# Forward and backward of four layers on one core: sweeps in alternating direction, three blocks kept in SBUF, and two turns of layer 2 done by DMA

## The chip, the core and the metric

The kernel runs on one core of a Trainium2 chip. Its time is the device time of one execution in microseconds. Of the kernel before, 8 runs are shown: median 1104.16 us, from 1103.3 to 1107.43.

## The reference

A network of four layers is applied to x (2048 tokens of 512 channels, bf16), and then the gradients of its input and of all five weights are computed from grad_out. The layers are A, B, A, B with the same weights for both As and both Bs; each adds its result to x. In the kernel they are layers 0, 1, 2 and 3.

```python
def _A_ref(x, wqkv, wo):          # 32 heads of 16 channels
    q, k, v = qkv[0], qkv[1], qkv[2]
    phi = lambda t: jnp.where(t > 0, t + 1, jnp.exp(t)) + 1e-6
    pq, pk = phi(q), phi(k)
    kv = jnp.einsum("bhsd,bhse->bhde", pk, v)
    z = jnp.einsum("bhsd->bhd", pk)
    num = jnp.einsum("bhqd,bhde->bhqe", pq, kv)
    den = jnp.einsum("bhqd,bhd->bhq", pq, z)[..., None] + 1e-6
    return (num / den) @ wo
def _B_ref(x, w_gate, w_up, w_down):   # 1376 hidden channels
    return (_sigmoid(x @ w_gate) * (x @ w_up)) @ w_down
x = x + _A_ref(_layernorm(x), ...); x = x + _B_ref(_layernorm(x), ...)   # twice
```

Two properties set the shape of the kernel. An A layer needs sums over all tokens (kv and z) before any token can go on, and so does its backward pass. So the tokens have to be walked through several times.

## The kernel before, in words

The 2048 tokens are cut into 8 blocks of 256. Five sweeps walk over the blocks, and a last stage computes the weight gradients:

1. Sweep 1: layer norm of layer 0 (h), K and phi(K), the sums G = h'pk and z, and Q (`a_k`, `a_q`). A barrier (`a_barrier`) forms kv and the matrix Wp = kv times wo.
2. Sweep 2: the second half of layer 0 (`a_p2`: 1/den, the normalised pnT = phi(q)/den, then ya = pn Wp), layer 1 (`glu_fwd`), and layer norm, K and sums of layer 2. A barrier again.
3. Sweep 3: Q of layer 2 and its second half (`a_p2`), layer 3 forward and backward together (`glu_both`), and the first backward half of layer 2 (`a_b1`: it needs the gradient dx turned, so that channels lie on partitions; dpn = gradient times WpT, and the sum M over all tokens). A backward barrier (`a_bbarrier`).
4. Sweep 4: the second backward half of layer 2 (`a_b2`), the backward pass of layer 1 (`glu_bwd`), the first backward half of layer 0.
5. Sweep 5: the second backward half of layer 0.
6. `dw`: gradients of the weights, as long products over all tokens (dw_ps).

All sweeps walk the blocks from 0 to 7. What a later sweep needs is stored to DRAM by block and loaded again: the f32 stream (xf_d loaded as x2l, dxa_d as dxal, dxb_d as dxbl), h, phi(k), pnT, rphiT (the derivative of phi over den), dqT, dkT.

The order of the instructions isn't that of the code. Each step is registered as a piece in a planner (`Plan`, lines 75 to 270) with its dependencies, the tokens (buffers) it takes and gives back, and an estimated cost on each engine; hand-set offsets (OFFSETS, lines 284 to 295) shift its priority. The planner runs the pieces against its own clock, and the order in which it starts them becomes each engine's order, which the chip follows: an instruction that isn't ready stops all that stands behind it on its engine. All DMAs are issued by SyncE (SP) in one such order. Pools limit what may lie in SBUF: t2 has 20 buffers of 256 KB (128x1024 bf16), xb has 5 of 512 KB (a block of the f32 stream), w4 7, w11 6; in PSUM there are five mm tiles, two acc tiles and one tp tile.

There are two ways to turn a tile. `add_turn` (line 484) turns half a block by four transposes on TensorE into PSUM (line 479) and one copy by ScalarE (line 481). `load_turn` (line 498) reads from DRAM with a transposing DMA.

1/den of a block lies as 128 tokens x 32 heads (`den`, line 806). Before the change VectorE writes it as two bf16 parts into rr (lines 822, 824), TensorE turns it (`turn`, line 826) and spreads each head's row over its 16 channels by a product with a constant matrix (`spread`, line 834, r_ps), and VectorE multiplies from PSUM: pnT = pqT times r (line 844) and rphiT (lines 847, 849). ya_ps (line 856) waits for both halves of pnT.

Further lines that matter: hTq is the turned h of layer 2 that Q of blocks 2 to 7 uses, loaded at line 773 (Q of blocks 0 and 1 uses the tile that K had). The gradient of layer 2 is cast by ScalarE (line 905) and turned by `add_turn` (line 943); dpn_ps (line 914) uses it, m_ps (line 963) doesn't. dha_ps (line 1129) uses dqTl. The backward layer norm `ln_bwd` (line 1058) is one step on ScalarE, one on VectorE, one on GpSimd (ab, line 1070) and two more on VectorE. wgT is loaded at lines 1486 and 1487; lines 1471 and 1488 clear the unused rows of wd, wuT and wgT on GpSimd.

Of the kernel before, what the change touches and what calls it, by code (L numbers as in the profile page):

```python
# [74 lines left out]
class Plan:  # L75
# [11 lines left out]
    RATE = 0.27  # L87
# [17 lines left out]
    def load(self, key, fn, mb, deps=(), use="", pull=0.0):  # L105
        self.add(key, fn, 0.0, deps, [("D", mb / self.RATE)], use, pull=pull)

# [172 lines left out]
ACCJ, ACCY = 11, 7  # L280
SUMS = {1: ([0, 1], -1), 3: ([2, 3], 1), 5: ([4, 5], 3), 6: ([6], 5), 7: ([7], 6)}
# [3 lines left out]
    CB1:1=-7 DE0:1=-63,2=-19,4=+5,7=+5 DE2:1=-23 DK0:2=+1,4=+21 DP0:0=+36,1=-28,2=+36,3=+36,5=-102 DP2:2=+63,6=-51  # L285
    DT0:+83 DW1:0=-30 DW3:1=+1,7=-2 E3:0=-31,1=+2 G11:0=-7,6=+24,7=+66 G3:1=+1 GS0:3=+31,5=-1,6=-86 GS2:5=+7,6=+44
    J0:1=-74 K0:3=-12 K2:0=+28,1=+28,2=+28,3=+28,4=+29,6=+44,7=+10 LB2:1=-93 LB3:2=-52,3=-12,6=+63,7=+106 LDH0:0=-49
    LDH2:3=+97 LDL0:0=+53,2=+38 LDP0:1=-6 LDP2:3=+41 LDQ0:3=+67 LDX0:0=+113 LDX2:1=-102,2=-13 LG3:0=+7 LH1:6=-75
    LN0:1=-131,5=-68,6=+58 LN2:0=-1 LP0:7=-44 LS1:1=-57 MS0:5=-40 MS2:1=-12,5=-34,7=-87
    Q0:1=-103,2=-115,4=-101,5=-22 Q2:0=-1,1=-23,2=+8 RT0:2=+7 RT2:2=+47 S0:+44 S2:-3 SG2:-64 SH1:2=+17 SN0:4=+50  # L290
    SP0:0=-66 SP2:1=-6,5=-11,7=+1 SPREAD:-24 SQ2:0=+2,6=-77 SU1:3=+1,6=-21 SV1:0=-15,3=+22,6=-13
    TG0:0=+6,1=+3,2=+7,4=+3,5=-18 TG2:6=+38 TK0:2=+113,5=+22,6=+48 TK2:7=+55 TR1:3=-11 UT0:2=-98,3=+2 WGT:-26
    WPL0:+56 WT0:0=-35,1=-40 Y33:7=-97 YA2:5=-43 ZE0:0=+1,3=-2 ZE2:2=+16,4=+19,6=+151 ZS0:5=-8,7=+136 ZS2:7=-52
    ZZ0:+35
# [7 lines left out]
def kernel(  # L302
# [38 lines left out]
    k.rphi_d = {l: dt_(f"rphi_d{l}", [D, S]) for l in (0, 2)}  # L341
# [156 lines left out]
def load_turn(k, key, src, put, name, deps, pull=0.0):  # L498

    def ld():  # L500
        t = t2(k, name)
        put(t)
        k.nc.sync.dma_start_transpose(out=t[:], in_=src)
    k.G.load(f"{key}.0", ld, BLK, deps, "+t2", pull)
    k.G.add(f"{key}.1", lambda: None, 0.0, [f"{key}.0"])


def layernorm(k, l, b, x_fn, deps, sums=False):

    nc, G = k.nc, k.G  # L510

    def half_sums(j):
# [3 lines left out]
        col = slice(2 * b + j, 2 * b + j + 1)  # L516
        rs, sx = k.rstd[l][:, col], k.sx[l][:, col]
# [18 lines left out]
    def half(j):  # L536
# [3 lines left out]
        col = slice(2 * b + j, 2 * b + j + 1)  # L540
# [24 lines left out]
    G.store(f"SH{l}.{b}", lambda: nc.sync.dma_start(out=tok3(k.h_d[l], b), in_=k.h[l, b][:]), BLK, [f"LN{l}.{b}.{j}@h" for j in range(2)])  # L565
# [15 lines left out]
def a_k(k, l, b, keep, by_dma=False):  # L581
# [3 lines left out]
    n = f"{l}.{b}"  # L585

# [9 lines left out]
    if by_dma:  # L596
        load_turn(k, f"TK{n}", k.h_d[l][brows(b), :], put, "hTk", [f"SH{n}"])
    else:
        add_turn(k, f"TK{n}", lambda: k.h[l, b], put, "hTk", [[f"LN{n}.{j}@h"] for j in range(2)])
# [5 lines left out]
    G.store(f"SPK{n}", lambda: nc.sync.dma_start(out=tok3(k.pk_d[l], b), in_=A.pk[b][:]), BLK, [f"K{n}.{j}" for j in range(2)])  # L605
# [160 lines left out]
def a_q(k, l, b, keep, deps):  # L766
    nc, G = k.nc, k.G
    A = k.A[l]
    n = f"{l}.{b}"

    def ld():
        A.hT[b] = t2(k, "hTq")
        nc.sync.dma_start_transpose(out=A.hT[b][:], in_=k.h_d[l][brows(b), :])

    def half(hf):
# [3 lines left out]
        for c2 in range(2):  # L779
            for m in range(NDC):  # L780
                nc.tensor.matmul(ps[:, c2, :], lhsT=k.wq[:, m, cslice(2 * hf + c2)], rhs=A.hT[b][:, m, :],  # L781
                                 start=(m == 0), stop=(m == NDC - 1))
        yield
        yield from phi(k, flat(A.pq[b][:, 2 * hf:2 * hf + 2, :]), flat(ps[:]))
    if keep:
        src = [f"TK{n}.0", f"TK{n}.1"]
    else:
        G.load(f"LQ{n}", ld, BLK, [f"SH{n}", f"<K{n}.1"] + deps, "+t2")
        src = [f"LQ{n}"]
# [3 lines left out]
    G.free("-t2", [f"<Q{n}.1", f"<K{n}.1"])  # L793


def a_p2(k, l, b, xin_fn, deps, late):
# [4 lines left out]
    n = f"{l}.{b}"  # L801

# [3 lines left out]
    def den():  # L806
# [9 lines left out]
        yield  # L816
        r = k.p1.tile([P, 2, H], F32, name="rcp", tag="rcp", bufs=2)
# [8 lines left out]
    def turn():  # L826
# [5 lines left out]
        nc.vector.tensor_copy(st["rT"][:], flat(tps[:]))  # L832

# [17 lines left out]
    def y(j):  # L851
# [3 lines left out]
        for c in range(NDC):  # L855
# [4 lines left out]
    G.load("LX" + n, lx, BLK if l == 0 else 2 * BLK, [f"YA{l}.{b - 2}.1", f"SX{l - 1}.{b}"] + deps, "+t2" if l == 0 else "+xb")  # L860
    G.add("DE" + n, den, 8 * 0.027, [f"Q{n}.0", f"Q{n}.1", f"ZZ{l}", f"<YA{l}.{b - 2}.1"],
          [("V", 0.22, "+dn -tp"), ("V", 0.55), ("V", 0.2, "+rr"), ("V", 0.22, "-dn")], "+tp")
    G.add("RT" + n, turn, 2 * C128, ["DE" + n, "SPREAD"] + late, [("V", 0.29, "-tp +rT")], "+tp -rr")
    for hf in range(2):
        G.add(f"SP{n}.{hf}", lambda hf=hf: spread(hf), 2 * C256, ["RT" + n] + ([f"<SP{n}.0"] if hf else []),
              [("V", 0.68, "@pn"), ("V", 0.29, "+s1"), ("V", 0.68, "-s1 -mm")], "+mm" if hf else "+mm +t2 +t2")
    pn = [f"SP{n}.{hf}@pn" for hf in range(2)]
    G.free("-rT", [f"<SP{n}.1"])
    G.free("-t2", [f"SP{n}.0", f"SP{n}.1"])
    G.store(f"SN{n}", lambda: nc.sync.dma_start(out=dmaj(k.pnT_d[l], b), in_=A.pn[b][:]), BLK, pn)  # L870
    G.store(f"SR{n}", lambda: nc.sync.dma_start(out=dmaj(k.rphi_d[l], b), in_=A.rphi[b][:]), BLK, [f"SP{n}.{hf}" for hf in range(2)], "-t2")
# [10 lines left out]
def a_b1(k, l, b, deps):  # L882

    nc, G = k.nc, k.G
# [22 lines left out]
    def dpn(hf):  # L907
# [31 lines left out]
    G.load("LN_" + n, ldt, BLK, [f"SN{n}", f"<MS{l}.{b - 2 if b % 2 else b - 3}.3", f"<DP{l}.{b - 2}.0"] + deps, "+t2")  # L939
# [3 lines left out]
    add_turn(k, f"TG{n}", lambda: st["g"], lambda t: st.__setitem__("gT", t), f"gT{l}", [[f"CA{n}.{j}"] for j in range(2)], pull)  # L943
# [8 lines left out]
    G.store(f"SQ{n}", lambda: nc.sync.dma_start(out=dmaj(k.dqT_d[l], b), in_=st["dq"][:]), BLK, [f"ZE{n}.{hf}" for hf in range(2)], "-t2")  # L952
    if b in MSUMS:
# [26 lines left out]
        G.free(" ".join(["-t2"] * 2 * len(bs)), [f"<MS{n}.3"] + [f"<TG{l}.{bb}.1" for bb in bs])  # L980
# [104 lines left out]
def a_b2(k, l, b, x_load, out, deps, out_use=""):  # L1085
# [4 lines left out]
    n = f"{l}.{b}"  # L1090

# [3 lines left out]
    def ldt(nm, src):  # L1095
        st[nm] = t2(k, nm)
        nc.sync.dma_start_transpose(out=st[nm][:], in_=src[brows(b), :])

    def ldq():
        st["dqT"] = t2(k, "dqTl")  # L1100
        nc.sync.dma_start(out=st["dqT"][:], in_=dmaj(k.dqT_d[l], b))

    def ldh():
        st["h"] = t2(k, "hl", [P, 2, D])
        nc.sync.dma_start(out=st["h"][:], in_=tok3(k.h_d[l], b))
# [26 lines left out]
    G.load("LDH" + n, lambda: ldt("hT", k.h_d[l]), BLK, pre, "+t2")  # L1132
    G.load("LDP" + n, lambda: ldt("pkT", k.pk_d[l]), BLK, pre, "+t2")
    G.load("LDQ" + n, ldq, BLK, pre + [f"SQ{n}"], "+t2")
    G.load("LDL" + n, ldh, BLK, pre, "+t2")
    G.load("LDX" + n, ldx, 2 * BLK, pre + [f"SDX{l + 1}.{b}"], "+xb")
# [4 lines left out]
    G.store(f"SK{n}", lambda: nc.sync.dma_start(out=dmaj(k.dkT_d[l], b), in_=st["dkT"][:]), BLK, [f"DK{n}.{hf}" for hf in range(2)])  # L1141
# [3 lines left out]
    add_lnb(k, l, b, lambda j: (st["ps", j][:], st["h"][:, j, :], st["x"][:, j, :], out(st["x"], j)),  # L1145
            [[f"DH{n}.{j}", "LDL" + n, "LDX" + n] for j in range(2)], "mm", out_use)
    G.free("-t2 -t2", [f"<DH{n}.1"])
# [40 lines left out]
def glu_fwd(k, l, b):  # L1188
# [3 lines left out]
    n = f"{l}.{b}"  # L1192
    x = k.x
# [35 lines left out]
    for p in range(NPAIR):  # L1229
# [5 lines left out]
        G.add(f"Y{n}.{p}", lambda p=p: y(p), q * 2 * C512, [f"G{n}.{p}@hh", "WD"] + ([f"<Y{n}.{p - 1}"] if p else []),  # L1235
              [("V", 0.77, "-acc @0"), ("V", 0.77, "-acc")] if p == NPAIR - 1 else [], "" if p else "+acc +acc")
    G.free("-t2", [f"<G{n}.5"])
    G.store("SHH" + n, lambda: store_hh(k, k.hh_d[l], b, st["hh"]), HHB, [f"G{n}.{p}@hh" for p in range(NPAIR)])
    G.store("SS" + n, lambda: nc.sync.dma_start(out=k.s2t_d[b], in_=st["s2t"][:].rearrange("p a c t -> p (a c t)")), 2 * HHB,
            [f"G{n}.{p}" for p in range(NPAIR)], "-w11")  # L1240
    G.store("SX" + n, lambda: nc.sync.dma_start(out=tok3(k.xf_d, b), in_=x[0, b][:]), 2 * BLK, [f"Y{n}.5"])
# [13 lines left out]
def add_dh(k, l, b, st, src):  # L1255
# [8 lines left out]
    for p in range(NPAIR):  # L1264
# [4 lines left out]
        G.store(f"SU{n}.{p}", lambda p=p: store_pair(k, k.du_d[l], b, p, st["pair"][p][0][:]), mb, [f"{src}{n}.{p}@u"])  # L1269
        G.store(f"SV{n}.{p}", lambda p=p: store_pair(k, k.dg_d[l], b, p, st["pair"][p][1][:]), mb, [f"{src}{n}.{p}"])  # L1270
# [3 lines left out]
def glu_both(k, l, b):  # L1274
# [57 lines left out]
    G.load("LG" + n, lg, BLK, [f"<G{l}.{b - 2}.5"] + (["WWD"] if early else [f"<G{l}.{b - 1}.2"]), "+t2")  # L1332
# [18 lines left out]
    add_dh(k, l, b, st, "G")  # L1351
# [482 lines left out]
```

## Time and profile before

| | us |
|---|---|
| median of 8 runs | 1104.16 |
| the profiled execution, its own time | 1104.03 |
| its span, from first to last instruction | 1102.2 |
| TensorE busy in the span | 1074.4 |
| mean granted TensorE clock | 0.998 |
| DMA queue q1, share of 16 engines | 86.8% |

The span is cut into stages where the work changes: sweep 1 to about 44 us, the turnover to sweep 2 to 68 us, sweep 2 to 235 us, the turnover to sweep 3 to 257 us, sweep 3 to 533 us, sweep 4 to 742 us, sweep 5 among weight gradients to 884 us, and weight gradients alone to the end. A row of the profile gives a group of instructions with its count, busy time and mean duration; the duration of a product on TensorE contains its pipeline, so that products which follow each other overlap, and the distance of their starts is what one costs. A line of waits names the engine and line that waited, who released it, the total in us, how often, and the longest. Idle time of an engine that is not the bottleneck costs nothing.

### The profile page before, as it was taken

The page shows a single profiled execution, that of the slowest core. Times are in us where ns is not written, and L with a number is a line of the kernel's source. Part 1 is how long each engine was busy: PE and PEld are TensorE (multiplying, and loading weights), DVE is VectorE, ACT ScalarE, POOL GpSimd, SP SyncE. Part 2 cuts the span into 40 slices and gives each one's busy share as a digit, 9 for nine tenths or more (in the row PEclk, how much of TensorE's full clock was granted, in tenths as well). Part 3 has the DMA queues.
Part 4 walks back from the last instruction along what each step waited for, and adds up shares of the span by engine and source line. Part 5 has one row for each costly group of instructions (what it writes and reads, how often), then busy time and mean ns, then how long its engine had stood idle before and what let it go on. Part 6 is the DMA issues. An engine that isn't in the chain of part 4 may idle for free.

```text
span 1102.2 us, 20100 instructions
## 1 busy us (share of the span) xinstructions
PE 1074.4 (97%) x7561; PEld 710.5 (64%) x7660; DVE 656.2 (60%) x1613; ACT 366.1 (33%) x733; POOL 154.8 (14%) x435
## 2 busy tenths in 40 slices
PE   7999999989999999999999999999999999999998
PEld 4667676667666666776665656665554456666787
DVE  6798978688776789767957576767755000000010
ACT  7655454455343334433244534341111000000010
POOL 4146564313121002000001000000000000000000
PEclk9999999999999999999999999999999999999999
DMA  7728996997788678865999999979999999999960
GB/s 246 252 81 277 241 311 190 305 200 187 201 211 178 178 190 208 188 168 152 272 250 255 244 261 280 252 202 255 257 251 271 268 227 227 221 252 222 208 148 20
DMA packets 490339, 242.72 MB, mean 220 GB/s; under 512 B 296225, under 2 KB 474625, under 8 KB 488193
## 3 DMA queue, kind: packets, MB, share of 16 engines
q1 hardware_dynamic: 490240, 241.43, 86.8%
q8 instruction: 60, 0.98, 0.4%
q14 instruction: 39, 0.31, 0.1%
HBM read 68.75 MB, written 100.43 MB: 153 GB/s over the span
## 4 chain that ended last, share of the span: by engine, by line
PE 90%; DMA 4%; DVE 3%; ACT 2%; issue 1%; SPq 0%; POOL 0%; ACTq 0%; DVEq 0%
PE dw_ps L1716 25%; PE dh_acc L1251 7%; PE g_ps L1181 7%; PE u_ps L1181 7%; PE dhh_ps L1181 6%; PE dha_ps L1129 6%; PE dh_acc L1249 6%; PE y_ps L1370 3%; PE y_acc L1222 3%; PE dpn_ps L914 2%; PE ya_ps L856 2%; PE m_ps L963 2%; PE k_ps L592 2%; PE q_ps L781 2%; PE dpk_ps L1113 2%; PE g_ps L618 2%
## 5 line engine op out<-in xcount | busy, mean ns | idle before, releaser
L1716 PE MATMUL dw_ps<-dw_set,h 128*128 128x352 bf16 (+2 forms) x1536 | 205.6, 297 | 0.0
L1716 PEld LDWEIGHTS <-h 128*128 128x128 bf16 x1536 | 150.3, 98 | 55.3
L1698 DVE TENSOR_SCALAR dw_o<-dw_ps 128x512 bf16<-128x512 f32 (+3 forms) x33 | 17.6, 540 | 234.0 <-PE dw_ps L1716 214.5
L1251 PE MATMUL dh_acc<-wgT,dg 128*128 128x512 bf16 x349 | 132.3, 379 | 1.9
L1249 PE MATMUL dh_acc<-wuT,du 128*128 128x512 bf16 x317 | 120.1, 379 | 0.2
L1696 ACT ACTIVATE dw_o<-dw_ps 128x512 bf16<-128x512 f32 (+4 forms) x34 | 16.2, 480 | 245.9 <-PE dw_ps L1716 211.0
L1181 PE MATMUL u_ps<-hT,wu 128*128 128x256 bf16 x704 | 92.5, 273 | 0.0
L1181 PE MATMUL g_ps<-hT,wg 128*128 128x256 bf16 x704 | 92.5, 272 | 0.0
L1181 PE MATMUL dhh_ps<-gT,wdT 128*128 128x256 bf16 x704 | 89.0, 274 | 0.9 <-ACT gT L481 0.7
L1070 POOL TENSOR_SCALAR ab<-c 128x2 f32<-128x2 f32 x64 | 18.6, 291 | 446.7 <-DVE lnb_j L1067 441.9
L1181 PEld LDWEIGHTS <-wg 128*128 128x128 bf16 x704 | 68.1, 98 | 20.3
L1716 PE MATMUL dw_ps<-g,dw_set 128*128 128x512 bf16 (+1 forms) x343 | 77.3, 379 | 3.2 <-DMA dw_set<-hh_d 1.6
L1181 PEld LDWEIGHTS <-wdT 128*128 128x128 bf16 x704 | 68.6, 98 | 12.8 <-issue 1.2
L1181 PEld LDWEIGHTS <-wu 128*128 128x128 bf16 x704 | 68.9, 98 | 8.0
L1716 PEld LDWEIGHTS <-dw_set 128*128 128x128 bf16 (+1 forms) x352 | 35.1, 100 | 42.1 <-DMA dw_set<-hh_d 1.9
L1251 PEld LDWEIGHTS <-dg 128*128 128x128 bf16 x352 | 34.4, 98 | 33.4
L1249 PEld LDWEIGHTS <-du 128*128 128x128 bf16 x352 | 34.4, 98 | 33.4
L1064 ACT ACTIVATE lnb_t<-dha_ps,rstd 128x512 f32<-128x512 f32 x32 | 22.0, 688 | 83.9 <-PE dha_ps L1129 49.4
L481 ACT COPY gT<-gT_ps 128x512 bf16<-128x512 bf16 x48 | 28.2, 587 | 59.8 <-PE gT_ps L479 58.3
L1304 ACT ACTIVATE th<-g_ps 128x512 f32<-128x512 f32 (+1 forms) x48 | 26.8, 557 | 53.7 <-PE g_ps L1181 47.2
L1211 DVE SCALAR_TENSOR_TENSOR hh<-th,u_ps 128x512 bf16<-128x512 f32 (+1 forms) x48 | 30.4, 638 | 19.7 <-ACT th L1206 13.7
L1222 PE MATMUL y_acc<-wd,hh 128*128 128x512 bf16 x165 | 41.5, 379 | 0.6
(201 smaller groups left out, 1840.9 us busy)
## 6 DMA issues: line engine op xcount, KB each, us to landing
s2t_d<-s2t SPq DMA_DIRECT2D x8, 1408.0 KB, 6.6
s2tl<-s2t_d SPq DMA_DIRECT2D x8, 1408.0 KB, 8.1
hh_d<-hh SPq DMA_DIRECT2D x16, 640.0 KB, 4.6
du_d<-du SPq DMA_DIRECT2D x80, 128.0 KB, 2.9
dg_d<-dg SPq DMA_DIRECT2D x80, 128.0 KB, 2.7
h_d<-h SPq DMA_DIRECT2D x32, 256.0 KB, 2.9
h<-h_d SPq DMA_DIRECT2D x18, 256.0 KB, 4.9
pk_d<-pk SPq DMA_DIRECT2D x16, 256.0 KB, 2.6
```

The source lines that it names most:

```text
L481: nc.scalar.copy(dst[:, :, tslice(j)], ps[:])
L592: nc.tensor.matmul(ps[:], lhsT=A.hT[b][:, m, tslice(j)], rhs=k.wk[:, m, :], start=(m == 0), stop=(m == NDC - 1))
L618: nc.tensor.matmul(ps[:], lhsT=k.h[l, bb][:, j, cslice(m)], rhs=A.pk[bb][:, j, :], start=(first and i == 0), stop=(last and i == len(its) ...
L1129: nc.tensor.matmul(ps[:], lhsT=lh[:, c, tslice(j)], rhs=rh[:, c, :], start=(i + c == 0), stop=(i == 2 and c == NDC - 1))
L1181: nc.tensor.matmul(ps[:, i, :], lhsT=w[:, m, fsl(fc)], rhs=rhsT[:, m, :], start=(m == 0), stop=(m == NDC - 1))
L1211: nc.vector.scalar_tensor_tensor(hh, th[:, 0:w], 1.0, flat(up[:])[:, 0:w], ALU.add, ALU.mult)
L1222: nc.tensor.matmul(st["acc"][j][:], lhsT=st["hh"][:, fc, tslice(j)], rhs=k.wd[:, fc, :], start=(fc == 0), stop=(fc == NFC - 1))
L1249: nc.tensor.matmul(acc[j][:], lhsT=du[:, i, tslice(j)], rhs=k.wuT[:, fc, :], start=(fc == 0), stop=False)
L1251: nc.tensor.matmul(acc[j][:], lhsT=dg[:, i, tslice(j)], rhs=k.wgT[:, fc, :], start=False, stop=(fc == NFC - 1))
L1304: nc.scalar.activation(th[:, 0:w], flat(gp[:])[:, 0:w], ACT.Tanh, scale=0.5)
L1370: nc.tensor.matmul(ps[:], lhsT=st["hh"][:, fc, tslice(j)], rhs=k.wd[:, fc, :], start=(fc == 0), stop=(fc == NFC - 1))
L1716: nc.tensor.matmul(ps, lhsT=lhs(s_), rhs=rhs(s_), start=(s_ == 0), stop=(s_ == 31))
```

## The change

- Sweeps 2 and 4 walk the blocks from 7 to 0; the other sweeps from 0 to 7. Each function gets B, the place of the block in the data, beside b, its place in the sweep. So a sweep begins with the block on which the one before ended.
- The last three blocks of a sweep stay in SBUF for the next: the f32 stream from sweep 2 to 3 (KEEPX), from 3 to 4 and from 4 to 5 (KEEP), and dqT of three blocks for both backward halves. Their stores and loads of the f32 stream go; dqT is still stored, since the weight gradients need it, but not loaded. The turned h of layer 2 is kept for Q of the first two blocks of sweep 3, now the last of sweep 2 (KEEPQ).
- The gradient of layer 2 is turned by DMA from SBUF to SBUF, in halves of 128x512 (SBT).
- 1/den of layer 2 is turned by DMA for blocks 2 to 7 (RDMA): GpSimd repeats each head's value over its 16 channels into a bf16 tile rx, DMA turns it into rTx, and VectorE multiplies from SBUF. Layer 0 keeps the old way (RDMA is 8 for it).
- rphi lies in DRAM with rows of 2 KB per partition instead of 512 bytes.
- The three clearing steps go from GpSimd to VectorE, as pieces of their own.
- The planner gets a rate of its own for transposing DMAs, and a new list of offsets, so the order moves everywhere.

```diff
-    RATE = 0.27
+    RATE, TURNED = 0.27, 0.235
...
+KEEP = (3, 3)
+KEEPX, KEEPQ = 3, 2
+RDMA = (8, 2)
+SBT = range(8)
...
+        if by_dma:
+            r = k.p1.tile([P, 2, H], F32, name="rcp", tag="rcp", bufs=2)
+            nc.vector.reciprocal(r[:], dn[:])
+            for j in range(2):
+                yield
+                st["rx", j] = s1(k, "rx")
+                src = r[:, j, :].unsqueeze(2).to_broadcast([P, H, D // H])
+                dst = st["rx", j][:].rearrange("p (h e) -> p h e", h=H)
+                if l == 0:
+                    nc.scalar.copy(dst, src)
+                else:
+                    nc.gpsimd.tensor_copy(dst, src)
+            return
...
+    def turn_by_dma(j):
+        if j == 0:
+            st["rT"] = t2(k, "rTx", [P, 2, NDC, P])
+        nc.sync.dma_start_transpose(out=st["rT"][:, j, :, :], in_=st["rx", j][:])
+
+    def spread_turned(hf):
...
+        nc.vector.tensor_tensor(by_tile(A.pn[b]), by_tile(A.pq[b]), rT, ALU.mult)
+        yield
+        rphi = by_tile(A.rphi[b])
+        nc.vector.tensor_scalar(rphi, by_tile(A.pq[b]), -EPS, 1.0, ALU.add, ALU.min)
+        yield
+        nc.vector.tensor_tensor(rphi, rphi, rT, ALU.mult)
...
+    if l == 2 and b in SBT:
+        def turn(j):
+            if j == 0:
+                st["gTt"] = t2(k, "gT2", [P, 2, NDC, P])
+                st["gT"] = lambda m: st["gTt"][:, :, m, :]
+            nc.sync.dma_start_transpose(out=st["gTt"][:, j, :, :], in_=st["g"][:, j, :])
...
+    if kept:
+        G.add("LDQ" + n, lambda: st.__setitem__("dqT", A.dq[b]["dq"]), 0.0, [f"ZE{l}.{C}.{hf}" for hf in range(2)])
+    else:
+        G.load("LDQ" + n, ldq, BLK, pre + [f"SQ{l}.{C}"], "+t2")
...
-    G.store("SX" + n, lambda: nc.sync.dma_start(out=tok3(k.xf_d, b), in_=x[0, b][:]), 2 * BLK, [f"Y{n}.5"])
+    if b < NBLK - KEEPX:
+        G.store("SX" + n, lambda: nc.sync.dma_start(out=tok3(k.xf_d, B), in_=x[0, b][:]), 2 * BLK, [f"Y{n}.5"])
...
-        nc.gpsimd.memset(t[0:NFC * P - F, NFC - 1, :], 0.0)
...
+def add_zero(k, key, get, dep):
+
+    k.G.add(key, lambda: k.nc.vector.memset(get()[0:NFC * P - F, NFC - 1, :], 0.0), 0.0, [dep], [("V", 0.3)])
```

## The prediction

> **What bounds the kernel now.** First the page's first part and its chain, to see which engine ends the span:
> ```profile
> PE 1074.4 (97%) x7561; PEld 710.5 (64%) x7660; DVE 656.2 (60%) x1613; ACT 366.1 (33%) x733; POOL 154.8 (14%) x435
> ...
> PE 90%; DMA 4%; DVE 3%; ACT 2%; issue 1%; SPq 0%; POOL 0%; ACTq 0%; DVEq 0%
> ```
> TensorE is busy for 1074.4 of 1102.2 us, so only two things make the kernel shorter: less TensorE work, or less of its 27.8 us of idle time. The view of TensorE's waits says what the idle time is made of:
> ```profile
> PE hTk_ps L479 <- ACT h L555: 6.9, 1, 6.9
> PE q_ps L781 <- DMA hTq<-h_d: 2.2, 1, 2.2
> PE dw_ps L1716 <- DMA dw_set<-hh_d: 1.6, 1, 1.6
> PE ya_ps L856 <- DVE rphiT L849: 1.3, 2, 0.7
> ...
> PE dpk_ps L1113 <- DMA hT<-h_d: 1.1, 2, 0.7
> ```
> The first is the start (nothing can be multiplied before the first block is loaded and normalised) and stays. The others are short and stand at the turnovers between sweeps. A table by windows, cut at the turnovers, puts them in place (columns: window, length, busy us of PE, PEld, DVE, ACT and POOL, granted clock, DMA share, GB/s):
> ```profile
> 44.40:67.60 23.20, 20.23 (x190) 14.89 (x192) 22.88 (x59) 13.88 (x28) 5.19 (x16) 1.00 0.55 162
> 67.60:235.40 167.80, 166.85 (x1286) 117.22 (x1303) 133.05 (x292) 85.87 (x168) 79.01 (x205) 1.00 0.83 239
> 235.40:257.00 21.60, 18.74 (x176) 14.31 (x177) 17.44 (x44) 13.30 (x27) 5.05 (x14) 0.92 1.00 203
> 257.00:533.00 276.00, 274.06 (x1952) 187.46 (x1981) 217.01 (x524) 102.89 (x206) 35.45 (x100) 1.00 0.75 187
> ...
> 742.00:884.00 142.00, 137.81 (x758) 72.95 (x770) 76.45 (x199) 20.37 (x46) 4.27 (x16) 1.00 1.11 261
> ```
> Inside a sweep TensorE runs without a gap (rows two and four). The turnover from sweep 1 to 2 loses 3.0 us with VectorE full (22.88 of 23.20); from 2 to 3 it loses 2.9 us and the clock falls; from 742 on 4.2 us go, with the DMA engines full.
>
> **Part 1: work taken from TensorE.** The gradient of layer 2 is turned by 8 blocks x 2 halves x 4 = 64 transposes, and 1/den for blocks 2 to 7 by 6 x 2 transposes and 6 x 4 spreading products of 256 columns. The timeline gives the pace (start, duration):
> ```profile
> 433.06 0.60 PE L841 MATMUL r_ps<-rT,spread 128*128 128x256 bf16 x4
> 433.49 0.38 PE L1249 MATMUL dh_acc<-wuT,du 128*128 128x512 bf16 x1
> ...
> 440.84 0.39 PE L479 MATMUL gT_ps<-ident,g 128*128 128x128 bf16 x4
> 441.06 1.03 PE L963 MATMUL m_ps<-pn,g 128*128 128x512 bf16 x3
> ```
> Durations overlap; the starts count. Four transposes hold TensorE for 0.22 us, four spreads for 0.43 us, two transposes for 0.11. Sum: 16 x 0.22 + 6 x (0.43 + 0.11) = 3.5 + 3.2 = **6.8 us**. The order of the changed kernel has exactly these 100 products less and no others, and TensorE has no gap in sweep 3, so all of it is on the path. The Trainium skill speaks against this move: VectorE: DVE Perf Modes, "The three transpose paths", gives 390 ns for a 128x128 transpose on TensorE and 1309 ns by DMA, and its "Rules for kernel authors" prefer TensorE where the result may go to PSUM. By its figure the 64 transposes would be worth 25 us; by the row's pace 55 ns each, 3.5 us. I take the row, since these stand in a full stream. The DMA price doesn't count in engine time here but as latency, below.
>
> Off the path: ScalarE loses 16 copies of 0.585 us (9.4 us); VectorE loses per block 0.20 + 0.22 + 0.29 + 2 x (0.68 + 0.29 + 0.68) = 4.0 and gets 2 x (0.42 + 0.29 + 0.42) = 2.3 (bf16 products from SBUF, nearest row L1424, 418 ns), 10 us less over six blocks. In sweep 3 neither is full, so I count nothing. GpSimd gets 12 copies that repeat 1/den (nearest row L1213, 620 ns; 7 us in sweep 3, where it is 35 of 276 us busy; a rstd or ab step behind a pair comes up to 1.2 us later). The three memsets move from GpSimd (515 ns) to VectorE, 0.1 to 0.5 us each: nothing. What is queued behind them waits for a weight load; VectorE's next weight step waits for the same load already.
>
> **Part 2: transfers that go.** Three blocks less of six 512 KB transfers (xf_d, x2l, dxa_d, dxal, dxb_d, dxbl) and 6 loads of dqTl: 18 x 0.52 + 6 x 0.26 = 11.0 MB less. Added: 28 transposes of 128 KB, 3.7 MB. At 957 us of DMA time (86.8% of the span) for 242.7 MB this is 43 us less and 14 us more. rphi in rows of 2 KB instead of 512 B costs at most the same. Most of what goes lies at the turnovers, the only places where a DMA ended a TensorE wait after 556 us: 0.47 + 1.64 + 0.68 = 2.8 us. I count two thirds, **1.8 us** (bounds 0 and 3.5).
>
> **Part 3: the turnover from sweep 2 to 3.** The 2.2 us wait is not a slow transfer. SyncE's queue shows why (start, issue time):
> ```profile
> 233.72 7.06 SPq L1486 DMA_TRANSPOSE wgT<-in_B_w_gate_dram  x1
> 240.84 1.25 SPq L1487 DMA_TRANSPOSE wgT<-in_B_w_gate_dram  x1
> 242.19 1.25 SPq L773 DMA_TRANSPOSE hTq<-h_d  x1
> ```
> The turned hTq stands behind 8.3 us of issuing wgT. In the changed order, Q of the first two blocks uses tiles kept from the end of sweep 2, and the first product with hTq comes 5.1 us of TensorE work after kv_ps (7.9 before), but the two Qs are now filler there; hTq still follows wgT, whose issue now starts before the last K. I expect the wait to go. It costs more than 2.2 us:
> ```profile
> 246.00:248.00 2.00, 1.81 (x12) 1.46 (x13) 0.95 (x1) 0.57 (x2) 1.81 (x3) 0.73 1.20 264
> 248.00:250.00 2.00, 2.00 (x13) 1.47 (x11) 0.61 (x3) 1.23 (x4) 1.47 (x7) 0.50 1.68 222
> 250.00:252.00 2.00, 2.00 (x18) 1.73 (x17) 0.89 (x3) 1.16 (x2) 0.46 (x3) 0.91 0.53 160
> ```
> The granted clock fell to 0.73, 0.50 and 0.91: 2 x (0.27 + 0.50 + 0.09) = 1.7 us. The Trainium skill (TensorE: Matmul & The Clock Gate, "HAM oscillation") asks only that gaps stay under about 3.4 us; by that rule this 2.2 us gap would cost no clock and be worth 2.2. The row shows the loss, so I take 2.2 + 1.7 = **3.9 us** (bounds 0 and 4.5).
>
> **Part 4: what becomes later.** (a) Sweep 2 now begins with block 7, so the two Q blocks that filled sweep 1 (from 19.9 us) can't run until the last K. VectorE's products up to the first hh rise by two pqT, a den and two rr steps, about 3 us, in the stage where it is full. Against this the last K ends up to 3.5 us sooner (four half blocks of Q, 0.87 us each, are no longer ahead of it). TensorE has 2.3 us more work in before its first g_ps. Net I take **+1 us** (bounds -2 and +3.5).
> (b) 1/den by DMA: den 0.28, dn 0.22, reciprocal 0.55, two copies 1.24, landing, two products 0.84, hops 0.4, SyncE and VectorE queues about 1.4: 4.9 us plus the landing. No row shows a transpose from SBUF; nearest is pkT, 256 KB in 4.1 us (3.2 to 5.4), issued in 1.2 to 1.5. The page above would have 1.3 us for a square, so that is no worse. 4.9 + 4.1 = 9.0 us. TensorE runs in order, and ya_ps stands 11.9, 10.2, 12.4 and 9.6 us of its work behind den for blocks 2, 5, 6 and 7 (30 and more for 3 and 4): covered by 0.6 us at the least. If that cover goes, each us is paid on TensorE and by all queued behind ya_ps.
> (c) The last gradient of sweep 3: from the end of dh_acc through lnb (0.69 + 0.69 + 0.29 + 0.75 + 0.74), a second half 0.7, cast 0.62, hops 0.6, landing 4.1 = 9.2 us; its dpn_ps stands 11.0 us later. Earlier blocks have 18 or more. On SyncE 28 issues of 0.6 to 1.3 us (half the bytes of pkT) are 17 to 36 us more in 290 us, of which it waits 149; du and dg stores behind a waiting transpose are delayed by its wait, and their pair buffers free later.
> For (b) and (c) together I take **+1 us** (bounds 0 and +6; a new wait can't give time back).
>
> **Sum.** -6.8 - 1.8 - 3.9 + 1 + 1 = -10.5. From the profiled execution's 1104.03 us (span 1102.2 and 1.8 around it; 0.1 from the median of 1104.16): **1093.5 us**.
>
> **Rivals.** *Work only* (25%): the idle time saved at the turnovers comes back as waits for ya_ps, the first g_ps and dpk_ps. Then only part 1 remains: 1104.0 - 6.8 = 1097.2, with 1096 to 1101 for what it leaves. For it speaks that the orders leave under 2 us of cover in several places; against it the lighter DMA load.
> *All turnovers closed* (15%): part 2 at 3.5, part 3 at 4.5, (a) at -2, (b, c) at 0: -16.8, or 1087.2. Against it speaks that VectorE stays full from 44 to 68 us.
> *Slow transposes from SBUF* (12%): if they land in L us, the four tight ya_ps wait 4 x (4.9 + L) - 44.1 in sum. Without my us for (b, c) the rest is 11.5 below before, so from L = 8.7 us on the kernel is slower; at 10 it waits 15.5 us and takes 1108. Against it: no transpose of this size took over 5.4 us in the pkT row, though pn reached 9.1 once, and sweep 3 has DMA to spare (0.75).
> The likeliest case has the remaining 48%. That the tiles aren't kept is excluded: the built order has 5 instead of 8 of each transfer.
>
> **Chances.** A measurement of this kernel tells about 0.2% (2.2 us) from no change. The likeliest and both faster cases make up 88%, of which some 4 points fall within 0.2%; slower keeps 10, same 6. The range leaves out the best few and most of the slow case: 1087 to 1103.5.
>
> **What would show it.** TensorE busy near 1067.6; gT_ps x128, r_ps x40; no wait of q_ps for hTq and a clock of 1.00 near 240 to 255 us; DMA share near 84%; rTx and gT from SBUF landing in 3 to 5 us; waits for pnT at ya_ps under 1 us each. Wrong if ya_ps or dpn_ps of sweep 3 shows waits of several us, or if TensorE's idle time before its first g_ps is over 13 us (8.1 + 3.0 now).

## The result and the profile after

The changed kernel takes 1095.7 us (median of 11 runs, 1093.8 to 1101.3); beside it, the kernel before took 1104.4 (31 runs). The ratio is 0.9926, with an interval from 0.9913 to 0.9939. The profiled execution took 1096.09 us, its span is 1094.3 us, 7.9 less than before. The forecast was 1093.5.

The page's first part and its chain, as shown of before:
```profile
PE 1067.3 (98%) x7464; PEld 703.0 (64%) x7560; DVE 649.0 (59%) x1598; ACT 358.5 (33%) x717; POOL 166.2 (15%) x444
...
PE 90%; DVE 4%; DMA 3%; ACT 2%; issue 1%; SPq 1%; POOL 0%; DVEq 0%; ACTq 0%
```
TensorE is 7.1 us less busy and still has 90% of the chain. Of the idle time, 27.8 us before, 27.0 are left: on balance nearly the whole gain is busy time that went. The stages below show what this balance hides. TensorE's waits say what became of the idle time:
```profile
PE hTk_ps L484 <- ACT h L561: 6.8, 1, 6.8
PE hTk_ps L484 <- ACT hTk L486: 2.1, 3, 0.8
PE dpk_ps L1190 <- DMA hT<-h_d: 1.8, 1, 1.8
PE ya_ps L902 <- DVE rphiT L895: 1.1, 1, 1.1
PE dw_ps L1819 <- DMA dw_set<-hh_d: 1.0, 1, 1.0
...
PE dpn_ps L976 <- DMA gT<-g: 0.6, 1, 0.6
```
The wait for hTq (2.2 us) is gone. In its place stand shorter ones: hTk in sweep 1 (0.8 before), ya_ps in the turnover from 2 to 3, and dpn_ps, which waits for a gradient turned by DMA. The windows, cut at the same events as before (last K, first g_ps of sweep 2, kv_ps, first g_ps of sweep 3; the last row starts 3 us earlier than that of before):
```profile
43.40:71.70 28.30, 25.82 (x250) 18.97 (x252) 26.98 (x71) 17.35 (x32) 3.17 (x12) 1.00 0.43 138
71.70:236.50 164.80, 163.90 (x1243) 114.43 (x1257) 128.32 (x283) 83.39 (x165) 80.95 (x206) 1.00 0.87 243
236.50:258.70 22.20, 20.57 (x202) 16.37 (x203) 19.99 (x53) 13.36 (x26) 3.37 (x12) 1.00 0.45 107
258.70:527.00 268.30, 265.79 (x1848) 179.03 (x1876) 208.58 (x505) 95.18 (x191) 46.66 (x112) 1.00 0.78 197
739.00:884.00 145.00, 142.12 (x777) 75.49 (x789) 71.26 (x176) 19.43 (x44) 3.91 (x16) 1.00 1.11 252
```
In the third row the clock is 1.00 (0.92 before) and the DMA share 0.45 (1.00 before): that turnover is what the change repaired. The first has VectorE nearly full, as before (26.98 of 28.30), and is 5.1 us longer because more of TensorE's work stands in it (25.82 busy, 20.23 before); its idle time is not longer (2.5, 3.0 before). In the last the DMA engines are as full as before (1.11).

Since the two kernels do different work between any two events, I compare lateness: the start of a product less all TensorE work that stands before it in the kernel's own order, at the pace of the trace's starts (all of it is 1072.5 us before, 1065.7 after). The lateness gained in each stage, in us:

| stage | before | after | pe_back | stores | both_back | no_turn_b |
|---|---|---|---|---|---|---|
| start to first g_ps of sweep 2 | 13.5 | 15.5 | 16.2 | 15.5 | 17.0 | 16.8 |
| to kv_ps of the turnover 2 to 3 | -0.4 | -0.4 | -0.4 | -0.4 | -0.4 | 0.9 |
| to first g_ps of sweep 3 | 4.5 | 1.9 | 1.9 | 2.9 | 2.4 | 0.6 |
| to first dpk_ps of sweep 4 | 1.5 | 2.7 | 1.5 | 3.0 | 1.4 | 1.3 |
| to the end | 10.6 | 8.9 | 7.2 | 11.3 | 11.7 | 8.3 |
| sum | 29.7 | 28.6 | 26.4 | 32.2 | 32.1 | 27.9 |

Runs that don't differ in sweep 1 scatter in the first row between 15.5 and 17.0, so a single figure there is good to about 1.5 us. In the last row, four runs below whose order and work from sweep 4 on are those of the changed kernel (phi_pool, no_min, act_casts, wgt_den) lie from 0.8 us below its figure to 1.1 above. After against before: -6.8 of work, +2.0, -2.6, +1.2, -1.7; together -7.9.

### The profile page after: what moved, and what is told of

The parts are those of the page before. It is cut to its first block, busy times and chain, and to the rows that moved or that the text cites. A ratio compares the mean times of both kernels' runs of the same rounds, so it can differ in the third digit from the quotient of the medians.

```text
span 1094.3 us, 19925 instructions
## 1 busy us (share of the span) xinstructions
PE 1067.3 (98%) x7464; PEld 703.0 (64%) x7560; DVE 649.0 (59%) x1598; ACT 358.5 (33%) x717; POOL 166.2 (15%) x444
## 3 DMA queue, kind: packets, MB, share of 16 engines
q1 hardware_dynamic: 485120, 234.09, 84.6%
## 4 chain that ended last, share of the span: by engine, by line
PE 90%; DVE 4%; DMA 3%; ACT 2%; issue 1%; SPq 1%; POOL 0%; DVEq 0%; ACTq 0%
PE dw_ps L1819 25%; PE dha_ps L1206 7%; PE g_ps L1265 7%; PE u_ps L1265 7%; PE dh_acc L1337 7%; PE dhh_ps L1265 6%; PE dh_acc L1335 6%; PE y_ps L1457 3%; PE y_acc L1307 3%; PE k_ps L599 2%; PE dpn_ps L976 2%; PE m_ps L1037 2%; PE dpk_ps L1190 2%; PE ya_ps L902 2%; PE q_ps L791 2%; PE g_ps L625 2%
## 5 line engine op out<-in xcount | busy, mean ns | idle before, releaser
L1335 PE MATMUL dh_acc<-wuT,du 128*128 128x512 bf16 x327 | 123.9, 379 | 0.4
L1144 POOL TENSOR_SCALAR ab<-c 128x2 f32<-128x2 f32 x64 | 22.3, 349 | 400.1 <-DVE lnb_j L1141 399.8
L1265 PEld LDWEIGHTS <-wdT 128*128 128x128 bf16 x704 | 68.4, 98 | 13.5 <-issue 1.5
L1510 DVE TENSOR_TENSOR du<-s2tl,dhh 128x512 bf16<-128x512 bf16 (+1 forms) x48 | 19.0, 401 | 45.0 <-ACT dhh L1505 44.0
L1296 DVE SCALAR_TENSOR_TENSOR hh<-th,u_ps 128x512 bf16<-128x512 f32 (+1 forms) x48 | 30.5, 637 | 17.2 <-ACT th L1291 11.3
```

The source lines that it names most:

```text
L1144: nc.gpsimd.tensor_scalar(ab[:], c12[:], -1.0 / D, 0.0, ALU.mult, ALU.add)
L1265: nc.tensor.matmul(ps[:, i, :], lhsT=w[:, m, fsl(fc)], rhs=rhsT[:, m, :], start=(m == 0), stop=(m == NDC - 1))
L1296: nc.vector.scalar_tensor_tensor(hh, th[:, 0:w], 1.0, flat(up[:])[:, 0:w], ALU.add, ALU.mult)
L1335: nc.tensor.matmul(acc[j][:], lhsT=du[:, i, tslice(j)], rhs=k.wuT[:, fc, :], start=(fc == 0), stop=False)
```

## Experiments

My theory after the result: the TensorE work is worth its 6.8 us; the spared transfers shorten the turnovers from sweep 2 on; the reversed order costs about 2 us at the turnover from 1 to 2; and some of the saved work comes back as waits. The rival: only the TensorE work counts, and keeping blocks is worth nothing. All experiments but no_turn_b and fill_b keep the planned order of the changed kernel. The ratios are to the kernel before and rest on all executions; the changed kernel's is 0.9926. A difference of spans compares one profiled execution with one other, and where the ratios give another size, it stands beside it.

**pe_back: the work put back.**
```diff
+        for i in range(4 if l == 2 else 0):        # in dpn, ahead of its first product
+            nc.tensor.matmul(ps[:, 0, 0:P], lhsT=A.WpT[:, i, 0:P], rhs=st["gTt"][:, 0, i, :], start=True, stop=True, ...)
+        for i in range(2 if by_dma else 0):        # in y, ahead of its first product
+            w = P if i else D
+            nc.tensor.matmul(ps[:, 0:w], lhsT=A.pn[b][:, i, tslice(j)], rhs=A.Wp[:, i, 0:w], start=True, stop=True)
```


> The changed kernel in its own order, with the TensorE time that the two turns took put back as products whose result the next product overwrites: 4 products of 128 columns ahead of each dpn_ps of layer 2 (16 x 0.22 us) and one of 512 and one of 128 ahead of each ya_ps of blocks 2 to 7 of layer 2 (12 x 0.27 us), 6.8 us in all; nothing else is added. If TensorE's work in sweep 3 is on the path and the change gained by that work, the time is the changed kernel's plus 6.8: about 1102.5 us, a ratio to the kernel before of 0.998 to 1.000. If sweep 3 has slack that only other engines fill (the gain came from the transfers and the lighter VectorE and ScalarE), it stays within 2 us of the changed kernel, below 1098.

Span 1098.9 us, ratio 0.9955 (0.9943 to 0.9967): 4.6 us more (3.2 by the ratios), between the two. By the table the missing 2.2 us are lateness that went: sweep 3 gives 1.2 back (its waits for DMA turns are only seen by the faster TensorE), and after sweep 3 the wait for hT at 825 us is gone. TensorE's waits after 540 us in pe_back:
```profile
PE dw_ps L1824 <- DMA dw_set<-hh_d: 1.9, 2, 1.1
PE dhh_ps L1270 <- ACT gT L486: 0.7, 1, 0.7
PE dh_acc L1342 <- DVE dg L1517: 0.2, 1, 0.2
```
So a third of the saved work (by the ratios half) is paid back as waits, most of them for DMA: TensorE arrives earlier and the DMA doesn't.

**ghost and ghost1: transfers at the places of the spared loads.**
```diff
+def ghost(k, src):
+    for i in range(2):                             # range(1) in ghost1
+        k.nc.sync.dma_start(out=tok3(k.ghost_d[i], 0), in_=src)
...
         if b < KEEPX:                              # and where dx is kept, twice
+            ghost(k, tok3(k.xf_d, last))
             return k.x[0, last - b]
```


> The changed kernel in its own order, with the removed f32 traffic put back as copies from DRAM to DRAM that nobody waits for: two of 512 KB for each of the nine kept blocks, where the block would have been loaded (9.4 MB, at the turnovers from sweep 2 to 3, 3 to 4 and 4 to 5). If the lighter DMA load is part of the gain, as the prediction had it, the time rises by 1 to 3 us and the DMA-ended waits of dpk_ps and dw_ps grow. If the kept blocks are worth nothing to the time, it stays within 0.5 us of the changed kernel (1095.7). If SyncE's queue is the tight one, the 18 issues of about 0.5 us show as later hT and gT and the rise is above 3 us.

Span 1112.7 us, ratio 1.0059 (1.0042 to 1.0076): 18.4 us more (14.7 by the ratios), the last of the three cases. TensorE's largest waits in it behind sweep 1, and VectorE's in 225 to 262 us:
```profile
PE wp_ps L723 <- DVE dn L833: 7.7, 1, 7.7
PE dw_ps L1828 <- DMA dw_set<-hh_d: 5.1, 2, 4.7
PE dpn_ps L982 <- DMA gT<-g: 4.5, 3, 2.7
```
```profile
DVE wgT L1587 <- DMA wgT<-in_B_w_gate_dram: 7.9, 1, 7.9
```
VectorE stood at the clearing of the gate weight's unused rows until the weight had landed, with dn behind it. SyncE's queue gives the reason; first the changed kernel, then ghost (start, issue time):
```profile
224.26 5.69 SPq L1574 DMA_TRANSPOSE wgT<-in_B_w_gate_dram  x1
229.99 1.25 SPq L1575 DMA_TRANSPOSE wgT<-in_B_w_gate_dram  x1
...
233.03 1.55 SPq L783 DMA_TRANSPOSE hTq<-h_d  x1
```
```profile
231.24 2.02 SPq L469 DMA_DIRECT2D ghost_d<-xf_d  x2
233.35 0.56 SPq L618 DMA_DIRECT2D pk_d<-pk  x1
233.96 9.71 SPq L1580 DMA_TRANSPOSE wgT<-in_B_w_gate_dram  x1
...
246.74 1.64 SPq L789 DMA_TRANSPOSE hTq<-h_d  x1
```
The same transposing DMA holds SyncE for 5.69 us in the one and 9.71 in the other, and begins 9.7 us later; hTq comes 13.7 us later. But the copies are not what I had called them, copies that nobody waits for. They share two scratch tensors, so that a copy waits for an earlier one, and SyncE waits with it (215 to 252 us):
```profile
SPq L469 <- DMA ghost_d<-xf_d: 3.9, 2, 3.0
```
Up to 3.9 us of the delay therefore come from the way in which the copies are written, and ghost makes the traffic look dearer than it is.

> As the run with eighteen copies, but one copy of 512 KB (DRAM to DRAM) at each of the nine places where a kept block would be loaded. There the transpose of the gate weight ended 13.7 us later than in the changed kernel on SyncE and TensorE waited 7.7 us for what follows it, so about 6 us of that delay were covered. If the cost has such a threshold, half the copies delay it by about 7 us and TensorE waits about 1 us there and 2 to 4 us at the two later turnovers: span 1096 to 1099. If the cost is proportional to the traffic, half of 18.4: 1103.5. If the cost comes from SyncE's issue time alone (0.6 us each, not the traffic), nine of them are under a microsecond in each turnover: below 1096.

Span 1098.8 us, ratio 0.9976 (0.9957 to 0.9995): 4.5 us more (5.5 by the ratios). VectorE waited 4.4 us for the gate weight and TensorE 4.0 behind it, not the 1 us that I had taken; hTq came 9.4 us later on SyncE's queue (242.38 us). Here too SyncE stood 3.8 us for an earlier copy. Half the copies cost a quarter (by the ratios over a third), but by the lateness this isn't a threshold at this turnover: it lost 4.9 us more than in the changed kernel, against 9.5 in ghost, which is half. At the later turnovers nine copies cost nothing that can be measured and eighteen 7.2 us; only there does a threshold show. In the changed kernel VectorE reached the clearing of wgT at 237.5 us and didn't wait.

**stores: the nine stores put back, each behind another DMA of its block.**
```diff
     def sh():
         nc.sync.dma_start(out=tok3(k.h_d[l], B), in_=k.h[l, b][:])
+        if l == 2 and b >= NBLK - KEEPX:
+            nc.sync.dma_start(out=tok3(k.xf_d, B), in_=x_fn()[:])
...     # the same for dx: behind the DMA of gT2 to dxa_d, behind the store of dqT to dxb_d
```


> The changed kernel with nine stores put back, in its own planned order: the three x blocks and the two times three gradient blocks that stay in SBUF are also written to DRAM (512 KB each), each right behind another DMA of its block near the end of its sweep; nothing reads them. TensorE's work is that of the changed kernel (1065.7 us by pace). If the TensorE work alone explains the gain, the DMA traffic near the turnovers is worth nothing at this size: span 1094 to 1096, ratio to the kernel before 0.992 to 0.994. If the spared traffic is what shortened the turnover from sweep 2 to 3 (2.6 us by the offsets), the transpose of the gate weight ends some 3 to 6 us later on SyncE and the span is 1097 to 1099. If each copy costs as in the run with eighteen of them (18.4 / 18 = 1.0 us each), 1103.

Span 1097.9 us, ratio 0.9969 (0.9953 to 0.9985): 3.6 us by the spans, 4.7 by the ratios. That is the second case: keeping blocks is worth something. TensorE's waits from 225 to 262 us show how:
```profile
PE q_ps L795 <- DVE phq L897: 1.4, 1, 1.4
PE q_ps L795 <- DMA hTq<-h_d: 0.9, 1, 0.9
```
The wait for hTq is back. On SyncE's queue:
```profile
226.55 7.13 SPq L1584 DMA_TRANSPOSE wgT<-in_B_w_gate_dram  x1
...
238.44 1.69 SPq L787 DMA_TRANSPOSE hTq<-h_d  x1
```
hTq is issued 5.4 us later than in the changed kernel: 2.3 us because the gate weight's transpose begins later, 1.4 because it takes longer (7.13 us; 7.06 before), 1.7 behind it. Later dpk_ps waits 3.2 us for hT instead of 1.8.

**both_back: both at once.** The edits of pe_back and stores together.

> The changed kernel, in its own planned order, with both put back at once: the 6.8 us of TensorE products in sweep 3 (overwritten, as in the run with products alone, which took 4.6 us of span) and the nine stores (3.6 us). If the two costs add up, the span is 1102.5 and the ratio to the kernel before about 1.000: then those two are the whole gain, net of what the rest costs. If the products only fill time in which TensorE waits for the stores' traffic anyway, the span is 1099 to 1100.5 (ratio 0.996 to 0.998).

Span 1104.6 us, ratio 1.0022 (1.0012 to 1.0033). The costs add up (10.3 us for 6.8 + 3.6) and pe_back's rebate doesn't recur: with the stores in the queue, TensorE waits for hTq (1.8 us) and hT (3.2) although it has more work. The gate weight's issue is not what delays hTq here:
```profile
228.67 5.92 SPq L1589 DMA_TRANSPOSE wgT<-in_B_w_gate_dram  x1
...
238.94 2.10 SPq L787 DMA_TRANSPOSE hTq<-h_d  x1
```
It takes hardly longer than in pe_back (5.74), but begins 3.3 us later, and hTq comes 4.8 us later than there (234.18). So the two parts, work and spared stores, are more than the whole gain; what the rest of the change costs is 1104.6 - 1102.2 = 2.4 us.

**no_turn_b: reversal and keeping alone.**
```diff
-RDMA = (8, 2)
-SBT = range(8)
+RDMA = (8, 8)
+SBT = ()
```
and a new list of offsets.

> Walking backwards and keeping blocks alone: the third layer's gradient and 1/den go back to TensorE (6.8 us more of its work, GpSimd and the DMA lose the 28 small transposes), with an order of work planned anew. Its own plan ends 6.3 us later than the changed kernel's. If the TensorE work is nearly the whole of the gain: span 1100.5 to 1102.5, ratio 0.998 to 1.001. If keeping blocks is worth as much as the nine stores cost (3.6 us) and turning by DMA had cost 1.2 us of waits: 1094.3 + 6.8 - 1.2 = 1099.9, ratio 0.997. If DMA turning was worth nothing, because sweep 3 is limited elsewhere: below 1097.

Span 1100.4 us, ratio 0.9996 (0.9982 to 1.0010), 6.1 us above the changed kernel (7.7 by the ratios): alone these edits bring nothing that can be measured. The last column of the table says why: against before, the turnover from 2 to 3 gives 3.9 us and the part after sweep 3 gives 2.3, but sweeps 1 and 2 take 3.3 and 1.3. The order was planned anew, so its stages aren't those of the changed kernel with one part taken out. The counterpart, turning by DMA without reversal and keeping, was not run.

**phi_pool, no_min and act_casts: the turnover from 1 to 2.** Three doses of VectorE work in the same place.
```diff
-    nc.vector.tensor_scalar(e[:], e[:], 1.0, EPS, ALU.min, ALU.add)   # phi
+    (eng or nc.vector).tensor_scalar(...)      # phi_pool: GpSimd for the first halves of layer-0 Q
+    if full: nc.vector.tensor_scalar(...)      # no_min: left out for all layer-0 Q
-        cp(k, m, A.GTb[:, m, :], A.GT[m][:])   # act_casts: GTb, Wp of layer 0, rT of its blocks 0 to 2
+        cp(k, m if l else 0, A.GTb[:, m, :], A.GT[m][:])
```


> The changed kernel in its own planned order; one small VectorE step (minimum and add, 128x512 in bf16, 284 ns) of every first half of a first-layer query block goes to GpSimd, which is idle from 40 to 60 us: eight such steps, 2.3 us of VectorE's 36.5 busy in 40 to 80. If VectorE's queue sets the turnover from sweep 1 to 2, TensorE's waits from 50 to 72 shrink by 1 to 2 us and the span is 1092 to 1093.5. If they come from the length of one chain, not from the queue, nothing is gained: 1094 to 1096, or more if GpSimd's step is slow.

Span 1100.8 us, ratio 0.9991 (0.9976 to 1.0005). GpSimd's step was nearly seven times as long as VectorE's:
```profile
L580 DVE TENSOR_SCALAR phi_e<-phi_e x56: 272/290/595, 12.0 to 424.4; 128x512 bf16<-128x512 bf16 x56
L580 POOL TENSOR_SCALAR phi_e<-phi_e x8: 1917/1918/1957, 42.4 to 69.6; 128x512 bf16<-128x512 bf16 x8
```
VectorE waited 6.9 us for these steps, and the first g_ps came 6.9 us later. Delay in that queue passes on to the end. It doesn't yet say that less work there helps.

> The changed kernel in its own planned order; the step with minimum and add (284 ns of VectorE, 128x512 in bf16) is left out for all sixteen half blocks of first-layer queries, so their feature map is the larger of 1 + q and exp(q); TensorE, the DMAs and everything else stay. In the run with eight of these steps on GpSimd VectorE's queue stood 6.9 us for them and the first product of sweep 2's feed-forward part came 6.9 us later, as against TensorE's work. If that queue sets the turnover from sweep 1 to 2, taking 4.5 us from it brings that product 2.5 to 4.5 us earlier and the span is 1090 to 1092. If the queue only mattered because a slow step had been put into it, the span stays at 1094 to 1095.

Span 1093.8 us, ratio 0.9915 (0.9897 to 0.9932). The first g_ps has a lateness of 14.4 us, 1.1 less than in the changed kernel, for 4.5 us less in the queue (without the minimum the kernel computes something else and serves for its time alone). That lies within the scatter of this row: VectorE's queue is at most part of the 2 us. At the end 0.5 us of it is left.

> The changed kernel in its own planned order; two casts of the first layer's key-value sum (GTb, 0.68 us each), two of its folded output weight (Wp, 0.7 us each) and the copies of 1/den's transposes of the first three blocks (0.26 us each) go from VectorE to ScalarE, which has some 8 us idle from 50 to 63 us: 3.5 us less in VectorE's queue. If that queue sets the turnover from sweep 1 to 2, the first product of sweep 2's feed-forward part comes 1.5 to 3 us earlier and the span is 1091 to 1093. If the longer ScalarE queue delays the chain through GTb and Wp instead, 1094 to 1096.

Span 1095.0 us, ratio 0.9918 (0.9893 to 0.9944). Lateness at the first g_ps 15.0 us (0.5 less), and at dpk_ps of sweep 5 23.8 instead of 22.9: no gain is left at the end. Neither interval is clear of the changed kernel's.

**fill_b: two blocks of Q back into sweep 1.**
```diff
-        a_q(k, 0, b, True, [] if b < 2 else [f"<K0.{last}.1"])
+        a_q(k, 0, b, True, [] if b > 5 else [f"<K0.{last}.1"])
```
and a new list of offsets. If Q as filler was what sweep 1 lacked, I expected up to 2 us back (1092.3 to 1093.5), otherwise 1094 to 1096. Span 1099.3 us, ratio 0.9980 (0.9968 to 0.9992): 5.0 us more, outside both. The first g_ps is 2.9 us later, as against TensorE's work, than in the changed kernel, and hTk waits 2.4 us in sweep 1 instead of 2.1. The outputs of this kernel are wrong, for a reason that isn't known, so it can't settle the question; it gives no support to the filler.

**wgt_den and ghost_wgt: is it VectorE that makes ghost slow?** In both, clearing and scaling wgT go from their own pieces into den of block 2.
```diff
             nc.vector.reciprocal(r[:], dn[:])
+            if b == RDMA[1]:
+                nc.vector.memset(k.wgT[0:NFC * P - F, NFC - 1, :], 0.0)
+                nc.vector.tensor_scalar(k.wgT[:], k.wgT[:], -0.5, None, ALU.mult)
```


> The changed kernel in its own planned order, but the two VectorE steps on the turned gate weight (the clearing of its unused rows, 0.27 us, and its scaling by -0.5, 1.60 us) are issued some 22 us later, behind the reciprocal of block 2 at 261 us, still ahead of the first product that uses the weight (266 us). VectorE has 1.9 us less in the turnover from sweep 2 to 3 and that much more just behind it. If VectorE's queue is what still makes ya_ps wait there (1.1 us), the first g_ps of sweep 3 comes 0.5 to 1.5 us earlier and the span is 1093 to 1094; if the first hidden products behind it then wait for VectorE instead, 1094 to 1096.

Span 1096.3 us, ratio 0.9961 (0.9949 to 0.9973), slower than the changed kernel. ya_ps still waits 1.1 us, and wpt_ps waits 1.7 us for ScalarE behind it. The two steps stood well where they were.

> The run with eighteen copies of 512 KB (span 1112.7), with the same two VectorE steps issued later as in the run beside it. There VectorE stood 7.9 us for the landing of the gate weight with the products for 1/den and the folded weight behind it, and TensorE 7.7 us, with the clock at 0.74 in 240 to 260. If the price of the copies is paid through VectorE's queue, most of that stall and the clock loss go: span 1101 to 1105. If TensorE would wait for the late transposes (hTq or the gate weight itself) anyway, 1109 to 1113.

Span 1113.7 us, ratio 1.0080 (1.0063 to 1.0098). My theory fell: nothing was won. TensorE's waits from 215 to 300 us:
```profile
PE q_ps L797 <- DMA hTq<-h_d: 6.7, 1, 6.7
PE wpt_ps L746 <- ACT th L1399: 1.7, 1, 1.7
```
VectorE no longer stands for the weight, and now q_ps waits 6.7 us for hTq. The cause lies one step further back, in SyncE's queue: everything behind the gate weight's transpose is late, and it depends on the order only which of its receivers TensorE meets first. It is the 2.2 us wait of the kernel before in a larger size.

## Why the prediction was right, and where it wasn't

The sum was -10.5 us, the span shows -7.9. The signs are all right. By its steps:

*Part 1, work (-6.8).* Right in size: exactly these 100 products went, and putting this much back costs 4.6 us alone and 6.7 beside the stores (1104.6 - 1097.9). "TensorE has no gap in sweep 3, so all of it is on the path" was too strong: with the work gone, gaps of 1.2 us appear there, and pe_back showed that a third of it or more can come back as waits. The weighed rule of the Trainium skill (VectorE: DVE Perf Modes, "The three transpose paths") would have had the 64 transposes worth 25 us, an estimate from its 390 ns; no_turn_b, with all 100 products on TensorE, is only 6.1 us longer. The pace of the row, 55 ns, was the one to take.

*Part 2, transfers (-1.8).* Near in size, wrong in its mechanism, so that the size is luck. From sweep 4 to the end 1.7 us went, by single traces that scatter there by about as much. But the waits ended by a DMA after 556 us, which I expected to shrink from 2.8 us, are 3.2 now (hT 1.8, dw_set 1.0, pn 0.4); TensorE comes earlier and the DMA share there is 1.11 as before. Of what went, 1.1 us is a wait for ScalarE's dw_o. The spared stores do count there: with them back, this stage loses 2.4 us more, beyond that scatter.

*Part 3, turnover 2 to 3 (-3.9).* The mechanism was right: the wait for hTq went, with the loss of clock behind it, and the runs with stores or copies bring it back through SyncE's queue. What I hadn't said is that the spared stores themselves bring hTq forward: by 5.4 us against stores, by 4.8 between pe_back and both_back. They do it by everything that stands ahead of hTq; a shorter issue of the gate weight is a small part (1.4 and 0.2 us). The size was too large by 1.3 us: -2.6, since ya_ps now waits 1.1 us for rphiT with VectorE full (19.99 of 22.20). In no_turn_b's order the turnover gives the full 3.9.

*Part 4(a), sweep 1 and its turnover (+1).* It measures +2.0 (up to 3.5 in the other runs with the same sweep 1). TensorE's idle time before the first g_ps is 12.1 us (71.68 less 59.59 busy) against 11.1; the other microsecond is products that took longer than the pace I gave them. The idle time is lost in sweep 1, not in the turnover: 9.6 us before the last K has ended against 8.1, then 2.5 against 3.0. The waits of hTk are 1.3 us longer; that the two Q blocks are missing there as filler is argued, and fill_b doesn't support it. VectorE's queue behind it counts for little: taking 4.5 us from it won 1.1, within the scatter. The relief that I set against this was too large: the last K products began 1.1 us sooner (42.38, 43.44 before), where I had allowed up to 3.5.

*Part 4(b, c), turns by DMA (+1).* It measures +1.2, but for another reason. The landing was better than I took:
```profile
L862 SPq DMA_TRANSPOSE rTx<-rx x12: 1194/1206/1363, 262.1 to 423.7; - x12
...
DMA to landing us min/median/max: 2.4/2.7/5.1
```
A median of 2.7 us against 4.1, so ya_ps never waited for rTx, and the rival of slow transposes from SBUF fell. The issue was worse: 1.2 us for 128 KB, as long as the 1.25 of a 256 KB turn from DRAM. The one wait for such a turn is dpn_ps for gT, 0.6 us; the largest wait of this stage has nothing to do with the turns, 0.8 us of u_ps for VectorE's dkvT (0.2 for U before).

*The rivals.* "Work only" (1097.2) is nearer to the time than the case that I thought likeliest, and its sum is almost what happened; but not for its reason. The spared stores are worth 3.6 us and more, and that is used up by sweeps 1 to 3. "All turnovers closed" failed at the first turnover. In "slow transposes" the landing from which the kernel would be slower is 9.0 us by the formula given there, not 8.7; the 2.7 measured are far from both.

*The signs.* PE busy 1067.3 (near 1067.6), no hTq wait, clock 1.00, DMA share 84.6% (near 84) all came; rTx landed a little sooner than the 3 to 5 us given. The sign of error, over 13 us idle before the first g_ps, did not come (12.1).

Open: whether another order with filler in sweep 1 would win its 2 us back (the one tried, fill_b, lost 5.0), and what the turns by DMA are worth without the kept blocks. No run here beats the changed kernel beyond its interval.

## What to carry to other kernels

A transfer is worth what stands behind it in its queue, not its own time: look for what stands ahead of a late transfer, and for what makes that late. Work taken from the bounding engine brings its full size only as long as its partners keep up: here 6.8 us of it were worth 6.7 between both_back and stores, but 4.6 between pe_back and the changed kernel, where the rest came back as waits. An edit that does "nothing alone" (0.9996) may still pay together with another; that it does here isn't shown, since the other was not run alone.

## What the runs showed of the hardware

- A large transposing DMA holds SyncE for a time that depends on what else is in the queue: the same gate weight took 5.54 to 5.74 us in four runs without the nine stores and the copies (wgt_den, no_turn_b, the changed kernel, pe_back), 7.06 before, 7.13 and 5.92 with the stores (stores, both_back), 7.90 in ghost1, and 9.71 and 9.43 behind four copies of 512 KB (ghost, ghost_wgt). The 5.92 shows that the stores alone don't set it; what does stays open.
- The length of a gap alone doesn't decide whether the clock falls. After a wait of 3.2 us in stores it was at half for 3.41 us, which cost 1.7 us; in ghost a gap of 2.75 us (536.2 to 539.0) cost no clock; in phi_pool no gap near 71 us was over 1.4 us and yet the clock halved:
```profile
782.93:786.34 3.41, 0.73 (x7) 0.67 (x8) 0.20 (x1) 0.00 (x0) 0.00 (x0) 1.00 1.05 185
786.34:789.75 3.41, 3.41 (x15) 1.99 (x14) 2.79 (x7) 0.00 (x0) 0.00 (x0) 0.50 1.16 232
```
```profile
534.29:537.70 3.41, 1.93 (x10) 0.72 (x8) 3.26 (x8) 0.00 (x0) 0.00 (x0) 1.00 1.33 279
537.70:541.11 3.41, 2.14 (x18) 1.78 (x19) 0.61 (x3) 0.00 (x0) 0.00 (x0) 1.00 0.86 344
541.11:544.53 3.42, 3.37 (x18) 1.76 (x18) 3.42 (x15) 0.00 (x0) 0.00 (x0) 1.00 1.34 177
```
```profile
71.27:74.68 3.41, 1.46 (x14) 0.97 (x13) 3.12 (x10) 2.21 (x5) 2.87 (x10) 1.00 0.02 5
74.68:78.09 3.41, 3.32 (x12) 1.49 (x12) 2.96 (x8) 2.70 (x6) 0.19 (x1) 0.50 0.55 183
```
  (stores, ghost, phi_pool.) In these traces the stretches at half clock last 3.41 us, or two or three times that (but for those at the end of the span), and where a trace has several, their starts lie whole multiples of 3.41 us apart. Cut by this grid, every window in which TensorE was idle for 1.91 us or more (behind the start of the span) was followed by such a stretch; while the clock was full, no window with 1.88 us or less was. The gap in ghost falls on two windows (1.48 and 1.27 us idle), the short ones in phi_pool add up to 1.95 in one. So it is partly chance whether a wait like the 2.2 us of the kernel before costs its 1.7 us of clock: of the 35 executions of that kernel taken beside both_back, 5 kept a mean clock of 1.00 (1101.1 us on average), 20 had 0.998 (1103.3) and 9 had 0.997 (1105.0). The bound of 3.4 us that the prediction took from the Trainium skill (TensorE: Matmul & The Clock Gate, "HAM oscillation") does not hold here: the 2.2 us wait before was followed by 0.73, 0.50 and 0.91 in the prediction's rows.
- On GpSimd a minimum and add on 128x512 bf16 took 1918 ns, while its s2t step of the same shape from f32 takes 664 ns on average.
